# The order of all work in a gated SSM-convolution and GLU kernel, laid out anew

## The chip, the cores and the metric

The kernel runs on one core of a Trainium2 chip. The core has five engines that each work through a queue of their own in order: TensorE (PE, with its weight loads PEld), VectorE (DVE), ScalarE (ACT), GpSimd (POOL) and SyncE (SP). SP and POOL issue the transfers between the chip's memory and the buffers on the core. The metric is the device time of one execution in microseconds, the median over several runs.

## The reference

The inputs are one sequence of 2048 rows by 512 columns (u, also used as x) and the weights of two branches, which a gate mixes:

```python
x = A_u
g = _sigmoid((x * gate_w).sum(-1, keepdims=True))
a = _A_ref(x, ...)     # diagonal SSM as a long convolution
b = _B_ref(x, B_w_gate, B_w_up, B_w_down)
return g * a + (1 - g) * b
```

Branch A has 512 channels with 128 complex states each. It builds a kernel of length 2048 for every channel and convolves it with the input:

```python
logdA, dB = dt * A, dt * Bc
P = jnp.exp(logdA[:, :, None] * l[None, None, :])
K = jnp.einsum("dn,dnl,dn->dl", Cc, P, dB).real
y = irfft(rfft(pad(u)) * rfft(pad(K)))[:L] + u * Dskip
```

Branch B is a gated linear unit of width 1792: `h = _sigmoid(x @ w_gate) * (x @ w_up)`, then `h @ w_down`.

## The kernel before

**The gated unit.** The 2048 rows are worked in two halves of two blocks of 512; the 1792 columns in 14 tiles of 128, in groups of 3, 4, 4 and 3. Every float32 operand is split into a high and a low part in a reduced format, and three products (high-high, high-low, low-high) are summed. `split` (L1022) does this for x, for the gate and up weights and for the down weights: it takes a staging buffer `st`, loads 256 KB into it from SP's queue, and its inner part `halves` has ScalarE write the high part (L1031) and VectorE the low part (L1032). `load_x` (L1008), `load_gu` (L1041) and `load_dn` (L1065) call it. `hidden` (L1083) runs the gate and up products on TensorE (L1098). `post` (L1137) has ScalarE take the tanh (L1141), VectorE multiply by the up product (L1143), and both split the result into `h` (L1147, L1148). `down` (L1153) multiplies `h` with the down weights into the bank `dps` (L1170), and `add` puts the result out: the first group by a store from SP, later ones by a store from POOL that adds in memory (L1194), the last two groups of the rows 8 to 15 by VectorE into a buffer that is read back and stored at the end (`take`, L912).

**The SSM kernel.** The channels are worked in 16 groups of 32, two to a table. `powers` (L484) and `angles` (L514) make sines, cosines and exponentials on ScalarE and VectorE; `magnitudes` (L533) builds one factor `B` of the kernel table, `tables` (L581) the other, `T`, by repeated doubling on VectorE (`double`, L561, with L575 to L577), and multiplies the two on TensorE in bursts of 128 small matmuls (`kps`, L619), one burst per group. `sort` copies the result, `second` (L631) does the first step of its Fourier transform (`wps`, L649), copies it into `kev` on ScalarE (L658) and stores 1 MB to `a_k` from SP (L661). Eight such stores are made, four for each half j of the channels.

**The convolution.** `rows` (L671) reads u, takes the gate's dot products (`dot`), does the first step of u's transform (`ups`) and stores to `a_u` (`urest`, L734). `passes` (L750) runs over j = 0 and 1. For j it waits until the four stores of that half are planned, and then in four rounds loads a part of `a_u` (four loads), does the second step (`ustep`, L804, `s2u`), loads parts of `a_k`, transforms and multiplies (`kstep`, L832, `s2k`, twice in a round), does the first step back (`inverse`, L866, `ips`), copies out (`evict`, L888) and stores to `b_s`. `finals` (L929) reads `b_s` back once a half's stores are done, and `last` (L944, `fps`) does the last step, scales by the gate and adds to the output, by POOL's adding stores or into the buffers of `take`.

**What sets the order.** Each of these is a Python generator that yields its next instruction (or short run of instructions) with the engine it goes to. `Plan.run` (L250) picks one at a time and appends it to that engine's queue; which one comes next is read from the string ORDER (L66). A letter stands for a pair of a kind of work and an engine through LETTERS and TURNS (L56, L57), and takes the first instruction of that kind that is pending for that engine. For work that may go to ScalarE or VectorE, the letter also chooses the engine. The plan's durations enter the program only where a free buffer is chosen. Letters that the text uses:

- Z `hidden` (six matmuls; the first eight three), a `down` (three matmuls), U `tables` on TensorE (128 small matmuls), l `second` on TensorE, n its store on SP, m its copies on ScalarE
- E, D, F loads of gate and up weights, of x and of down weights on SP; f/g, d/e, h/i their splits on ScalarE/VectorE
- S `tables`, Q `mags`, N `angles`, K `powers` on VectorE; R, P, M `mags`, `angles`, `powers` on ScalarE
- u/v `post` on ScalarE/VectorE; y `add` on POOL; z `add` on VectorE; r/s `urest` copies on ScalarE/VectorE
- b loads of `passes` on SP; 1 `ustep`, 5 `kstep`, 8 `inv`, & `last` on TensorE; 2/3 `ustep` copies, !/# `evict` copies, (/) `last` on ScalarE/VectorE; 6 `kstep` on VectorE; $ `evict` stores and 9 loads of `finals` on SP; * `last` on POOL; c `take` on SP

Of the kernel before, what the change touches and what calls it, by code (L numbers as in the profile page):

```python
# [33 lines left out]
L, D, F = 2048, 512, 1792  # L34
# [29 lines left out]
         "kstep -", "kstep PE", "kstep DVE", "inv -", "inv PE", "finals SP", "evict ACT", "evict DVE",  # L64
         "evict SP", "last -", "last PE", "last ACT", "last DVE", "last POOL")
ORDER = (  # L66
    "ABDdeEfgZZEfGDdBgeZZEfgDdeZGVEfZBgDdeZWZWEfpgZZFDEudWfgZZhepvpAuvEWfEgZZDfCHugZZHpqXDIDJvIFdeZuKFdeiuhadeZKZLZMKvivahZMZ"
    "MNOMMGPXVEfKMuNPviuaSZwSZxPSSSvuSSZSPYVSvSSuQgRSSaaZZaEZfvwZgZauaSaSvRQrtxHuEZQZQvQwZtZaaSuuENOZPaZfvSNxSSTfrYVgEutPwKvE"
    "tWWUZZPvGHffPoaKLMQgZZZgZEKppuvuMRWWfpFuZvZaEfRpqMvMgZaZQQQuMurQTNOwUPZZKNMSutSvShoaaSaPSPSivSSuSZZPwaaaZZuSrgQRESjkwlvg"
    "StaaxaESxFRESxmfxQZwZfhaQQivvugQtmZZFhExgSNOSuPfZZavvuNnviZSgaZFEEhPituvaSSPZTwyUPuoZaaXQaIaRJXVIKHKwyZaRQLafMKaafZguwyv"  # L70
    "gUaaZaMQMYVQQNfZaOZTMuMKrvtvPNMwyuvSgSSKSKrZtEEYZtVtWWPWSSWuvPoaaaaZSjkPLSQSfrtMKtwyaupSpSZRSvMSfRQQQSSQSggNaaZurawtMZMy"
    "lmamtaZaOawyZZuESvvaZFPNpSphiSTavXFEaPuauZwyZPUPQXvZuvRZRQQQhQuFTZMKZoZhEENOVYZZVHrFtutrUvtMSPNSoZtfgfgSjSfZuvSZSiigaPkS"
    "hvPYVaZSuWZSPuvQSRRviSaaZSpSQwynZrWutWErtEttWQSfSZagZvQpuaaQSpNpSOawylaaaaZmuPNwPyZSPfaaXaSTawyPmZXVZUQogIvZuaaaJIKKaYst"
    "tZRwyaaaaLMKRQQQQrNTOVMfvnMtHZMwyMKgYPNUotauMSSKSSPSZPSZrPaDDSDjtSakrluZtZKvQSRRvSZZaSvZSQtZmmQdtQuvDuQNOnbbbbbb0veSuZwa"
    "ayavZZZPuNdePFuP1bb2ZSSvShvuaSiSdPFZSTZLM3ewUy45uKMFdhohvvubeZZaZZQRR6bub4MbZbH5iavZqDia6QZbQQQNOTuZMMPDdwyUZ6NKvPvMSSSS"
    "oaaSSubDdeajSZPSkuPdlZ6Swaa7eZuQSSmabbmb8DdnyRveSeZv!RSZZvE0!$wa$ZuuSQQQQSNOS!!$$ESyZaaw1baaaP2ZZuNPSSTwUbv345vZyPEbvZfg"
    "PQoaaaZZuvR6bRIbJ4u6bIKQbZbuQKLMywZaQaa5fgwQKMZaaT6MvaNObyM67wZU8fMKPoavqyNMaaSKZSSSjkPZSgwEaFaKxaEGfSub!vSuZ!$$SPSSgbyw"
    "aaPZSuQZSaS!b!x$vvSRlZRQQuvufQQSZwamLMKaaZmuNEMhOf0Sw1b$b3MSxZPNMgSvaZxaaZ24SgvZ56bbEPPTb4wbUZPZQuMuZZboababRRu5Z6ZaivEv"
    "KQbZQZbEbQQTv6xNOEwU67fgx8ZuMnPfNoaufaaZSSSSvgS!uZSP!$$vSvPwaaSaZSZESPSQgFuvhixSjSfFuvZSRZRgZQuvS!hQkQ!FhlZiQiZufgwaaamv"
    "NamnZSwaaaOPNP$aESuvP$SST0wP1bbZyZxUQuvoRRQQQQZaa2fgaZaZTuvZ34ZwUoj5bEb66akuvbb4auvaZawlmmnbbbbZZZuvbab56aZZyfEug6bvbbbZ"  # L80
    "7b8E#u!Eb#b$b$bav#Zfgbawuv013344$Zaaa56$56b66bZbb9buZE9bZy90bZafwbb71bb3g9Zu24bay8!b!Z$ZEfvf#4v#g%$05b66bEaZbZuE5bbg6vbb"
    "b&($bbZ)bb)f((**(6(**gZ0Za199f22a99Z$ZwauFaugv193399a7fvuEFaZu8!#4Z9hvg4Z$!%u$i%#5F&(6))((**fZZEbvu$f(h6g$999g(w&))b5v**"
    "ZiZuZb4Zav)((*9%*((hy**FcZha667iZbu&()i5)((**ca((**bcbZazZcaa6avaz8!!!6$aaaazZc#v4Z566$aubauauy7Zaz8a!ya$v#u$c!av!aZzaav"
    "$$Zavu$azZu$999aaa9%ZZc&()aycZaZua9aFaF)v(v(**F999%&9h99u(9%&ia(*zvvu(h*vhiazia99aaaa()aaza)(a(az)z*99))c)%&a)c)cz(ca)a)"
    "z)c)*aaaa(a(a*z))acaazczc*")

XLATE = 0
SLACK = dict(dma=1.6, eng=0.06)
# [226 lines left out]
def body(ctx, tc, xp, xt, prm, ldt, dsk, gw, wgu, wdn, c_wu, c_wf, c_wk, c_wwk, c_wwu, c_wwv, c_pw, out):  # L315
# [53 lines left out]
    g = cst.tile([P, NM], F32, name="g")  # L369
# [10 lines left out]
    E = {n: Ev() for n in ("dt", "pw", "wu", "gwb", "wk", "wf", "dsk")}  # L380
# [627 lines left out]
    def load_x():  # L1008
        for half in range(2):
            for sb in range(2):  # L1010
                if (half, sb) == (0, 1):
                    yield begun_w[0, XLATE]
                xsl, = yield X_, 1
                x = xsl.tile("x")
                xready[half, sb][1] = x, xsl
                o = half * HALF + sb * 512
                for dc in range(NC):
                    if (half, sb, dc) == (0, 0, 1):
                        yield first_w
                    yield from split("split", xt[dc, :, o:o + 512], x[:, 0, dc], x[:, 1, dc], xsl, xready[half, sb][0][dc])  # L1020

    def split(kind, src, hi, lo, slot, ready):  # L1022

        s, = yield ST, 1
        n = math.prod(hi.shape[1:])
        flat = s.tile("st")[:, :n]
        st = flat if len(hi.shape) == 2 else flat.rearrange("p (a b) -> p a b", a=hi.shape[1])
        t = yield "SP", kb(n / 2), lambda: S.dma_start(flat if len(src.shape) == 2 else st, src), [s.t]

        def halves():  # L1030
            te = yield "ACT", act(n) + 0.04, lambda: A.activation(hi, st, AF.Copy), [t, slot.t]  # L1031
            te = yield "DVE", dve(n), lambda: V.tensor_tensor(lo, st, hi.bitcast(F32), op=OP.subtract), [te]  # L1032
            s.free(te)
            ready.set(te)
        plan.spawn(halves(), kind)

    def drop(slot, used):
        yield used
        slot.free(used.t)

    def load_gu():  # L1041
        for half in range(2):
            for n, f in enumerate(SLICES[half]):
                if half == 1 and n < KEEP:
                    wready[1, f][1] = wready[0, f][1]
                    for k in range(2):
                        wready[1, f][0][k].set(0.0)
                    plan.spawn(drop(wready[1, f][1][1], wready[1, f][2]), "free")
                    continue
                gs, = yield GUW, 1  # L1050
                gu = gs.tile("gu")
                wready[half, f][1] = gu, gs
                if half == 1 or n < NF - KEEP:
                    plan.spawn(drop(gs, wready[half, f][2]), "free")
                for k, ready in enumerate(wready[half, f][0]):
                    if (half, f) == (0, 0):
                        src = wgu[f].rearrange("p (k c m) -> p k c m", k=2, c=NC)[:, :, k]
                        yield from split("splitw", src, gu[:, 0, :, k], gu[:, 1, :, k], gs, ready)
                        if k == 0:
                            first_w.set(0.0)  # L1060
                        continue
                    yield from split("splitw", wgu[f, :, 512 * k:512 * k + 512], gu[:, 0, k], gu[:, 1, k], gs, ready)
                begun_w[half, f].set(0.0)
# [138 lines left out]
    for gen, kind in ((steps(), "steps"), (const("pw", pw, c_pw.to_broadcast([P, NA + NS + 32]), kb(490)), "pw"),  # L1202
                      (load_x(), "x"), (load_gu(), "w"), (load_dn(), "dn"), (const("wu", wu, c_wu.rearrange("p (c r k) -> p c r k", c=2, r=2), kb(64)), "const"),
                      (const("gwb", gwb, gw.to_broadcast([P, D]), kb(560)), "const"), (preludes(), "preludes"), (powers(), "powers"),
                      (angles(), "angles"), (magnitudes(), "mags"), (tables(), "tables"),
                      (rows(), "rows"), (const("wk", wk, c_wk, kb(128)), "const"),
                      (const("dsk", dskt, dsk.rearrange("p (g s) -> p g s", g=NG), kb(64)), "const"),
                      (const("wf", wf, c_wf.rearrange("p (q m) -> p q m", q=2), kb(32)), "const"), (hidden(), "hidden"), (down(), "down"), (passes(), "passes"), *((take(t), "take") for t in range(8, NM))):
        plan.spawn(gen, kind)
# [58 lines left out]
```

## Time and profile before

| What | Value |
|---|---|
| Median of 3 runs | 648.88 us (645.97 to 654.21) |
| Profiled execution | 644.45 us |
| Its span, first to last instruction | 642.7 us |
| Mean granted TensorE clock | 0.984 |
| Bytes moved by transfers | 105.50 MB, mean 164 GB/s |
| Matmuls of `hidden` (L1098) and `down` (L1170) | 1344 and 672 |

The span is cut into 40 slices of 16 us in the page's second part, where each digit is the busy share of a slice in tenths. A wait is idle time of an engine just before an instruction, with what ended it. A window row sums an engine's busy time between two points of the span. The DMA share is the mean busy share of the core's 16 DMA engines, as the view prints it (it can read a little above 1).

### The profile page before, as it was taken

The page shows a single profiled execution, that of the slowest core. Times are in us where ns is not written, and L with a number is a line of the kernel's source. Part 1 is how long each engine was busy: PE and PEld are TensorE (multiplying, and loading weights), DVE is VectorE, ACT ScalarE, POOL GpSimd, SP SyncE. Part 2 cuts the span into 40 slices and gives each one's busy share as a digit, 9 for nine tenths or more (in the row PEclk, how much of TensorE's full clock was granted, in tenths as well). Part 3 has the DMA queues.
Part 4 walks back from the last instruction along what each step waited for, and adds up shares of the span by engine and source line. Part 5 has one row for each costly group of instructions (what it writes and reads, how often), then busy time and mean ns, then how long its engine had stood idle before and what let it go on. Part 6 is the DMA issues. An engine that isn't in the chain of part 4 may idle for free.

```text
span 642.7 us, 16774 instructions
## 1 busy us (share of the span) xinstructions
PE 603.5 (94%) x7145; PEld 451.9 (70%) x7145; DVE 548.5 (85%) x784; ACT 431.3 (67%) x650; POOL 49.9 (8%) x61
## 2 busy tenths in 40 slices
PE   7999989899998997998999999989999987998987
PEld 3667778677876875866776777767776664676755
DVE  5999889999999999999999899998657652985367
ACT  4595998789898599789966899587642332442130
POOL 0000000011100110000010100000100010242021
PEclk9999999999999899899999999999999987999989
DMA  7504624439634628589488346735489999998986
GB/s 246 174 33 115 197 68 160 143 48 229 149 100 157 164 35 234 161 179 210 96 165 173 69 124 157 217 105 156 72 193 253 233 240 276 256 208 187 239 177 164
DMA packets 94650, 105.50 MB, mean 164 GB/s; under 512 B 39664, under 2 KB 65136, under 8 KB 93552
## 3 DMA queue, kind: packets, MB, share of 16 engines
q1 hardware_dynamic: 86512, 92.89, 53.1%
q0 software_dynamic: 8064, 11.54, 13.0%
q8 instruction: 56, 0.92, 0.6%
q14 instruction: 18, 0.15, 0.1%
HBM read 61.41 MB, written 42.99 MB: 162 GB/s over the span
## 4 chain that ended last, share of the span: by engine, by line
DVE 37%; PE 24%; ACT 14%; DMA 13%; issue 7%; SPq 4%; POOL 1%; DVEq 0%; POOLq 0%; ACTq 0%
PE gups L1098 10%; PE dps L1170 9%; DVE t L575 3%; DVE T L576 3%; DMA parts<-b_s 3%; DVE T L577 3%; DVE h L1148 2%; DVE sg L1143 2%; DVE gu L1032 2%; ACT B L547 2%; DMA parts<-a_u 2%; DVE B L556 2%; DMA st<-wgu 2%; DVE dnw L1032 2%; DVE ex L475 2%
## 5 line engine op out<-in xcount | busy, mean ns | idle before, releaser
L1098 PE MATMUL gups<-x,gu 128*128 128x512 f32 x1344 | 338.2, 399 | 5.7 <-ACT sg L1141 1.5
L1098 PEld LDWEIGHTS gups<-x,gu 128*128 128x128 f32 x1344 | 251.4, 190 | 77.3 <-issue 8.5
L1170 PE MATMUL dps<-dnw,h 128*128 128x512 f32 x672 | 176.8, 400 | 6.0 <-DVE h L1148 2.8
L1170 PEld LDWEIGHTS dps<-dnw,h 128*128 128x128 f32 x672 | 125.6, 190 | 45.2 <-issue 7.5
L1194 POOL DMA_DIRECT2D out<-part x31 | 27.8, 896 | 452.1 <-ACT part L1189 437.9
L1147 ACT ACTIVATE h<-sg 128x512 fp32r<-128x512 f32 x56 | 34.7, 627 | 32.7 <-DVE sg L1143 18.6
L547 ACT ACTIVATE B<-B 128x32 f32<-128x32 f32 (+2 forms) x96 | 53.5, 672 | 0.3
L1189 ACT ACTIVATE part<-dps,omg 128x512 f32<-128x512 f32 x47 | 32.0, 682 | 22.6 <-PE dps L1170 22.4
L1148 DVE TENSOR_TENSOR h<-sg,h 128x512 fp32r<-128x512 f32 x56 | 38.2, 684 | 7.6 <-ACT h L1147 7.5
L575 DVE TENSOR_TENSOR t<-T,bz 128x1024 f32<-128x1024 f32 (+3 forms) x48 | 41.2, 859 | 1.9 <-ACT ez L479 0.7
L577 DVE TENSOR_TENSOR T<-T,t 128x1024 f32<-128x1024 f32 (+3 forms) x48 | 41.5, 864 | 0.7
L1143 DVE SCALAR_TENSOR_TENSOR sg<-sg,gups 128x512 f32<-128x512 f32 x56 | 37.5, 679 | 5.3 <-ACT sg L1141 5.3
L576 DVE TENSOR_TENSOR T<-T,bz 128x1024 f32<-128x1024 f32 (+3 forms) x48 | 41.3, 860 | 0.0
L619 PEld LDWEIGHTS kps<-B,T 128*32 128x32 f32 x2048 | 29.4, 110 | 12.2 <-ACT part L1189 9.7
L1031 ACT ACTIVATE gu<-st 128x512 fp32r<-128x512 f32 (+1 forms) x49 | 29.1, 606 | 12.2 <-DMA st<-wgu 12.0
L619 PE MATMUL kps<-B,T 128*32 128x64 f32 x2048 | 31.9, 220 | 5.3 <-ACT part L1189 4.9
L1032 DVE TENSOR_TENSOR gu<-st,gu 128x512 fp32r<-128x512 f32 (+1 forms) x49 | 32.0, 661 | 3.0 <-ACT gu L1031 3.0
L1141 ACT ACTIVATE sg<-gups 128x512 f32<-128x512 f32 x56 | 33.1, 591 | 0.8 <-PE gups L1098 0.6
L658 ACT ACTIVATE kev<-wps 128x1024 f32<-128x1024 f32 x16 | 30.9, 2003 | 3.1 <-PE wps L649 3.1
L340 ACT ACTIVATE ev<-ips 128x512 f32<-128x512 f32 x23 | 13.2, 597 | 27.9 <-PE ips L879 19.9
L479 ACT ACT_TABLE_LOAD x23 | 29.5, 1283 | 0.4
L340 ACT ACTIVATE yt<-fps 128x512 f32<-128x512 f32 x7 | 4.2, 597 | 32.2 <-PE fps L954 32.2
(129 smaller groups left out, 728.7 us busy)
## 6 DMA issues: line engine op xcount, KB each, us to landing
st<-wgu SPq DMA_DIRECT2D x45, 256.0 KB, 4.8
a_u<-evu SPq DMA_DIRECT2D x32, 256.0 KB, 4.3
a_k<-kev SPq DMA_DIRECT2D x8, 1024.0 KB, 4.9
b_s<-ev SPq DMA_DIRECT2D x32, 256.0 KB, 4.4
out<-part POOLq DMA_DIRECT2D x31, 256.0 KB, 4.4
ak<-a_k SPq DMA_DIRECT2D x28, 256.0 KB, 6.1
parts<-b_s SPq DMA_DIRECT2D x24, 256.0 KB, 8.0
st<-wdn SPq DMA_DIRECT2D x23, 256.0 KB, 4.7
```

The source lines that it names most:

```text
L547: A.activation(B[:, :, 0, 1 << k::2 << k], B[:, :, 0, 1:64 >> k:2], AF.Exp, scale=float(1 << k))
L575: yield "DVE", c, lambda: V.tensor_tensor(t2, src, sb, op=OP.mult), [t, slot.t]
L576: te = yield "DVE", c, lambda: V.tensor_tensor(dst, src, br, op=OP.mult), [t]
L577: te = yield "DVE", c, lambda: V.tensor_tensor(dst, dst, t2[:, :, ::-1], op=OP.add), [te]
L619: mm(p[32 * jj:32 * jj + 32, s], T[:, 32 * i + ch, c], B[:, ch, c], start=(c == 0), stop=(c == 1), tile_position=(0, 32 * jj), skip_group_ ...
L1032: te = yield "DVE", dve(n), lambda: V.tensor_tensor(lo, st, hi.bitcast(F32), op=OP.subtract), [te]
L1098: mm(p, gu[:, a, k, dc], x[:, b, dc], start=(dc + n == 0), stop=(dc == NC - 1 and n == 2))
L1141: t = yield "ACT", ("exp", actp(512)), lambda: A.activation(sg, pg_, AF.Tanh, scale=0.5), [tg, ss.t]
L1143: t = yield "DVE", dve(512), lambda: V.scalar_tensor_tensor(sg, sg, 1.0, pu, op0=OP.add, op1=OP.mult), [t, tu]
L1147: t = yield "ACT", act(512), lambda: A.activation(h[:, 0], sg, AF.Copy), [t, hs.t]
L1148: t = yield "DVE", dve(512), lambda: V.tensor_tensor(h[:, 1], sg, h[:, 0].bitcast(F32), op=OP.subtract), [t]
L1170: mm(p, h[:, a, 128 * s:128 * s + 128], dn[:, b], start=(f == fs[0] and n == 0), stop=(f == fs[-1] and n == 2))
```

## The change

ORDER is replaced as a whole by another string of the same length; the operations stay the same. In `split`, the number of elements is no longer taken from the shape of the destination but from a new argument, 512 unless given, and `load_gu` gives 256 for the four pieces of the first block. That number sets the size of the staging buffer and of the load, and the durations with which the plan books the two halves of the split. Of both strings the last lines are shown, from the line with the sixteenth U on; the thirteen lines ahead of them are left out.

```diff
 ORDER = (
...
-    "NamnZSwaaaOPNP$aESuvP$SST0wP1bbZyZxUQuvoRRQQQQZaa2fgaZaZTuvZ34ZwUoj5bEb66akuvbb4auvaZawlmmnbbbbZZZuvbab56aZZyfEug6bvbbbZ"
-    "7b8E#u!Eb#b$b$bav#Zfgbawuv013344$Zaaa56$56b66bZbb9buZE9bZy90bZafwbb71bb3g9Zu24bay8!b!Z$ZEfvf#4v#g%$05b66bEaZbZuE5bbg6vbb"
-    "b&($bbZ)bb)f((**(6(**gZ0Za199f22a99Z$ZwauFaugv193399a7fvuEFaZu8!#4Z9hvg4Z$!%u$i%#5F&(6))((**fZZEbvu$f(h6g$999g(w&))b5v**"
-    "ZiZuZb4Zav)((*9%*((hy**FcZha667iZbu&()i5)((**ca((**bcbZazZcaa6avaz8!!!6$aaaazZc#v4Z566$aubauauy7Zaz8a!ya$v#u$c!av!aZzaav"
-    "$$Zavu$azZu$999aaa9%ZZc&()aycZaZua9aFaF)v(v(**F999%&9h99u(9%&ia(*zvvu(h*vhiazia99aaaa()aaza)(a(az)z*99))c)%&a)c)cz(ca)a)"
-    "z)c)*aaaa(a(a*z))acaazczc*")
...
+    "OfmSSZwyamnZaZP1bbNSSSaPZSgTPawUuPQgvZuEZoaRaRQQaZQEQTya2fEuZv345bbbwyb6E6Uo$Zvj$kaaa4ufauwlmgZZaZZ5vgmavuZZuEEnbbbbbbbb"
+    "b6bbybv67Z8!##a0bawZuf#v13Z244f5vu656Z$b$bbbb6Za67$$b0uZaZa8f!!!bZuEg9bv#gf1999b%$3vbZb24$b56g&(v))awbZb4(fb6gZZuva56(*6"
+    "*Eb0b9$Z(bb9bbb(*a*aZa1$fwgb32456ZgZ6E7b8!E#au!v9uv4ZF9%au!vb$Zfg$9$hifZ9Fb9&))b5b9Zu$60Zau)(9(**((*v6Fb9ga99huvviZZ%w12"
+    "*Zu%&(b3v)Z)((b4FZaa**&)(hi(*Zb7aZ*))hZ5((bciZ6uvZa**((8!z!aaZ**b46acyaz!!$56$6b7aaaZa8cz$#!c$$a$uv!!$uvaya$cuvZ9caZyzaa"
+    "cuaazvZ9aaauaZvuz9aavaaz9%&)y)Z)9a9cu9ZaFhi(9%(*9F9hai*F&)((*azvhi9Zu*9%)aa9a9aaa9vu&()9(av(zz)a)aa)ca%z*a)a)c&zc)caaa(a"
+    "*())))a)azc)azcaaazcazc(**")
...
@@ -1019,10 +1019,9 @@
                         yield first_w
                     yield from split("split", xt[dc, :, o:o + 512], x[:, 0, dc], x[:, 1, dc], xsl, xready[half, sb][0][dc])
 
-    def split(kind, src, hi, lo, slot, ready):
+    def split(kind, src, hi, lo, slot, ready, n=512):
 
         s, = yield ST, 1
-        n = math.prod(hi.shape[1:])
         flat = s.tile("st")[:, :n]
         st = flat if len(hi.shape) == 2 else flat.rearrange("p (a b) -> p a b", a=hi.shape[1])
         t = yield "SP", kb(n / 2), lambda: S.dma_start(flat if len(src.shape) == 2 else st, src), [s.t]
@@ -1055,7 +1054,7 @@
                 for k, ready in enumerate(wready[half, f][0]):
                     if (half, f) == (0, 0):
                         src = wgu[f].rearrange("p (k c m) -> p k c m", k=2, c=NC)[:, :, k]
-                        yield from split("splitw", src, gu[:, 0, :, k], gu[:, 1, :, k], gs, ready)
+                        yield from split("splitw", src, gu[:, 0, :, k], gu[:, 1, :, k], gs, ready, 256)
                         if k == 0:
                             first_w.set(0.0)
                         continue
```

More of the change, by code (lines that the diff above doesn't have):

```diff
@@ L66 @@
 ORDER = (
[L67 to L78, printed above, removed]
@@ L79 @@
-    "KQbZQZbEbQQTv6xNOEwU67fgx8ZuMnPfNoaufaaZSSSSvgS!uZSP!$$vSvPwaaSaZSZESPSQgFuvhixSjSfFuvZSRZRgZQuvS!hQkQ!FhlZiQiZufgwaaamv"
-    "NamnZSwaaaOPNP$aESuvP$SST0wP1bbZyZxUQuvoRRQQQQZaa2fgaZaZTuvZ34ZwUoj5bEb66akuvbb4auvaZawlmmnbbbbZZZuvbab56aZZyfEug6bvbbbZ"
-    "7b8E#u!Eb#b$b$bav#Zfgbawuv013344$Zaaa56$56b66bZbb9buZE9bZy90bZafwbb71bb3g9Zu24bay8!b!Z$ZEfvf#4v#g%$05b66bEaZbZuE5bbg6vbb"
-    "b&($bbZ)bb)f((**(6(**gZ0Za199f22a99Z$ZwauFaugv193399a7fvuEFaZu8!#4Z9hvg4Z$!%u$i%#5F&(6))((**fZZEbvu$f(h6g$999g(w&))b5v**"
@@ L83 @@
-    "ZiZuZb4Zav)((*9%*((hy**FcZha667iZbu&()i5)((**ca((**bcbZazZcaa6avaz8!!!6$aaaazZc#v4Z566$aubauauy7Zaz8a!ya$v#u$c!av!aZzaav"
-    "$$Zavu$azZu$999aaa9%ZZc&()aycZaZua9aFaF)v(v(**F999%&9h99u(9%&ia(*zvvu(h*vhiazia99aaaa()aaza)(a(az)z*99))c)%&a)c)cz(ca)a)"
-    "z)c)*aaaa(a(a*z))acaazczc*")
+    "ABEfgBDdeZZEGfDdBgeZZEfDdGVWpeWpEfWgZDdZpgeZZWpXAEfgDdZZEefguZZqvuEFHHCIJvDhfdIiaKgZEfZuKLMKMFvgZZeZDdMuXFNOVYeMDhMKdPeZ"
+    "viauZZvZEMZhNEuSViSSvaSPuZvZPurPttfrYSuZwaaaEtFfStZSVKWvWKSSQRSZRgSSvLMwaaaSgGHZSQZEufxErtWQKMMQSZQvNEWHxwaaauZZOuZZPfMS"
@@ new lines @@
+    "hfSpSNPvZZSTgvwUZuvpgPGZxpxEufPQuZRgpvRZvZigqoaaaQZruuZQQQTvvNOtwEtMKufUgPNMSSSZufvSgSEZSoPaaavSSZPZEtPuQSZvuZSRvZjSuSZR"
+    "QkQwaaaQvZuQSwxNOlaaFaFhhZvPxFSiSNZEZSfwaufhvxEiPZuSXvPamgZaZZZSiEuPEvfZuSTawyZUxXVmfYgZgVQoIaZrutaagJIHKKRvLMvKaRQQQQNO"
+    "wyuvMZMMaaaawyfgMKPTZNauaaawyHfgvZUZMSSSEnturtZYVPKSKLoaaPMaErtSaSvSjWWkZSfWPSWuKSQpgSSvZSrlwyRZRQQQQMSNOuvpaZZaaaSmMZmt"
+    "wytPuZtEvpESapNaauvaZSSwyaaFFfgMPSTafPFaPuvhiZZZZFwyUZXQhiuvoZRaZZEEZXVRQQfuvufZZMQhihiuvYVvaaZQuTuvvawygtUNOPKMgNSfZrtt"
@@ new lines @@
+    "gSSoSjSSSgkaSZSrYttVWPWWPZPEEaaSQWaSSuvnwyZSRRpQSQQrQpZatautaaSwyZNvOSpSSaaaZrtlPmfNpSauvXgXwyTZfZaPaZaaZPuwUmZPQouZnIJa"
+    "aVyYRgIvKKLaZtRQMKZDruDtQMaZDZQQvdTMwyUMNOMPvKeNDodMSudeSPrZtvVPSKSjkSStKPuSeZaSSvSQYaaawyruRZSaRFShvSQaiFtatFtQZQZaQHud"
+    "vZrNOuevwyZhhlmmZPSNiSiuZZZZaaSLSDdttuZZPuSPMKDdPSTawyvZvMvUQMeDnbbbbbb01bbdMDeuvMKeZRRQQQQuv2ZoZMuNOZaa245b6bb4qbbHaTbZ"
+    "dZwyPNUP5bbboaZ6baSjkPSPu6aSQRSRveSwyS6SQSlmSQS7vQZmuvQSNZOaZaZaEEfwuv8!F!$$0SyuvfSaZPgSZSNhSaawyuvZSaSaiST!!q12bb$2ZZEP"
@@ new lines @@
+    "Zu4awyEgZP5bbbbbbb4U6PQZuEovavIa6Ra$JwIyZuRQQaKuKvfZaZ5bZEbabZuLMKQMMMQTn6wZyMZUNfOPKZugNMSgfSSZ67SvSoSjaaaPPvkPQSvSwx8!"
+    "!u$Z$SgRESaaKaZSZRQQQSvZ!SQZuSwxaaEaNSOfu0!wxlZa$aamZmn1bbKPuSZNSZSgSTwUxfvg2EvvPP245LMKbbb4bPQuv6Zfgoaauav6ZRRQQwMuZMZx"
+    "bEMaQQNO$MKa5awbxbvbZfaPaNfgau6ZTwUbPZMSxZ678PSSSvSoSaPQauFbgZSajvZ!!0$$hSSiRuSvSRQQk!ZZwFauvQ!ZFhSiZauhiZluvQxGEfaaSEvN"
+    "OfmSSZwyamnZaZP1bbNSSSaPZSgTPawUuPQgvZuEZoaRaRQQaZQEQTya2fEuZv345bbbwyb6E6Uo$Zvj$kaaa4ufauwlmgZZaZZ5vgmavuZZuEEnbbbbbbbb"
```

## The prediction

> **What bounds the kernel now.** I read the page first, then the windows by stage, then the timeline of TensorE in the last stage, then the groups for prices. The page:
>
> ```profile
> span 642.7 us, 16774 instructions
> PE 603.5 (94%) x7145; PEld 451.9 (70%) x7145; DVE 548.5 (85%) x784; ACT 431.3 (67%) x650; POOL 49.9 (8%) x61
> DVE  5999889999999999999999899998657652985367
> ACT  4595998789898599789966899587642332442130
> DMA  7504624439634628589488346735489999998986
> ```
>
> Two stages show. In the first 70% of the span VectorE is full, slice after slice, and DMA is half idle; then VectorE falls off and DMA is full. TensorE's 94% says little: its busy time runs on while a matmul waits for its weights. Windows cut at the last table group and the last `wps` group say it in numbers (busy us and count of PE, PEld, DVE, ACT, POOL; clock; DMA share; GB/s):
>
> ```profile
> 20.00:440.00 420.00, 401.23 (x4916) 308.75 (x4915) 407.18 (x573) 351.50 (x518) 21.02 (x24) 0.99 0.54 139
> 440.00:462.00 22.00, 20.86 (x271) 16.14 (x269) 15.38 (x16) 16.27 (x23) 2.61 (x3) 1.00 0.65 149
> 470.00:591.00 121.00, 112.59 (x1412) 78.56 (x1397) 77.46 (x102) 40.41 (x70) 18.53 (x21) 0.96 1.05 231
> 591.00:643.00 52.00, 45.23 (x290) 32.91 (x289) 29.41 (x48) 12.19 (x24) 7.03 (x8) 0.96 0.80 196
> ```
>
> From 20 to 440 us VectorE idles 420 - 407.2 = 12.8 us, and from 440 to 462 another 6.6. So the sixteenth table group (letter U), which needs all tables, comes when VectorE has got through what stands before it. From 470 to 591 us the DMA share is 1.05: the second half of the passes (j=1), its reads and writes and the output, is held by transfers. The landmarks in the timeline of TensorE, with its waits for transfers:
>
> ```profile
> 461.98 1.99 PE L619 MATMUL kps<-B,T 128*32 128x64 f32 x128
> 469.23 2.10 PE L649 MATMUL wps<-wk,kst 32*64 32x128 f32 x128
> 502.21 0.71 PE L817 MATMUL s2u<-parts,wwu 32*32 32x256 f32 x28 [0.54 <-DMA parts<-a_u]
> 518.67 0.66 PE L954 MATMUL fps<-parts,wf 64*32 64x256 f32 x14 [2.62 <-DMA parts<-b_s]
> 534.36 0.62 PE L817 MATMUL s2u<-parts,wwu 32*32 32x256 f32 x4 [2.02 <-DMA parts<-a_u]
> 535.36 0.71 PE L817 MATMUL s2u<-parts,wwu 32*32 32x256 f32 x28 [0.39 <-DMA parts<-a_u]
> 536.62 0.87 PE L817 MATMUL s2u<-parts,wwu 32*32 32x256 f32 x4 [0.54 <-DMA parts<-a_u]
> 537.76 1.15 PE L817 MATMUL s2u<-parts,wwu 32*32 32x256 f32 x28 [0.27 <-DMA parts<-a_u]
> 618.76 1.10 PE L954 MATMUL fps<-parts,wf 64*32 64x256 f32 x14 [0.77 <-DMA parts<-b_s]
> 630.33 8.45 PE L1170 MATMUL dps<-dnw,h 128*128 128x512 f32 x36
> ```
>
> U16 runs at 462.0 us, the last `wps` (l8) at 469.2 us, and some 173 us follow it.
>
> **The change part by part.** The new argument of `split` gives the value that the removed line worked out (512, and 256 for the first block of gate and up weights), so the two edits there alter no instruction. What remains is the order string. Counted letter by letter, both strings have 2186 letters and the same number of each, apart from the engine of a few copies: `urest` one from VectorE to ScalarE, `ustep` four from VectorE to ScalarE, `evict` three from VectorE to ScalarE, `last` three from ScalarE to VectorE. So nothing is added; the cost lies in where things stand. The prices:
>
> ```profile
> L340 DVE COPY uf<-s2u 128x1024 f32<-128x1024 f32 x4 | 4.9, 1217 | 0.0
> L340 DVE COPY evu<-ups 128x1024 f32<-128x1024 f32 x1 | 1.2, 1224 | 0.0
> L340 ACT ACTIVATE uf<-s2u 128x1024 f32<-128x1024 f32 x6 | 6.0, 1016 | 2.4 <-issue 1.8 <-PE s2u L817 0.6
> L855 DVE TENSOR_TENSOR uf<-s2k,uf 128x1024 f32<-128x1024 f32 x10 | 12.2, 1224 | 0.3
> L861 DVE TENSOR_TENSOR uf<-tt 128x512 f32<-128x512 f32 x10 | 6.9, 692 | 0.3
> L1143 DVE SCALAR_TENSOR_TENSOR sg<-sg,gups 128x512 f32<-128x512 f32 x56 | 37.5, 679 | 5.3 <-ACT sg L1141 5.3
> ```
>
> (1) VectorE ahead of U16. Before minus after, by letters ahead of the sixteenth U: `ustep` copies 4 become 1 (-3 x 1.22 = -3.66), the `urest` copy goes (-1.22), one `post` instruction moves behind (-0.68), and one whole `kstep` product moves ahead (two instructions of 1.22 and two of 0.69: +3.83). Sum -1.7 us on the engine that sets this stage, on the path. ScalarE gets there three `ustep` copies, one `urest` copy of 1.02 each and one split more, +4.7 us; in 20 to 440 it is idle 420 - 351.5 = 68.5 us, which hides it. If that cover failed, the 4.7 would fall on VectorE's waits.
>
> (2) VectorE's idle time in that stage. Its waits before 460 us are small ones for ScalarE:
>
> ```profile
> DVE B L552 <- ACT B L547: 3.6, 3, 2.9
> DVE ex L475 <- ACT af L474: 2.6, 2, 1.5
> DVE B L541 <- PE kps L619: 2.0, 1, 2.0
> ```
>
> The new order interleaves `mags`, `angles` and `powers` on ScalarE in another way, and no row shows which waits come of it. Bounds: all idle time of 20 to 462 goes, -19.4; as much again comes, +19.4. The longest single row is 2.9 us, and the same producers and consumers stay, so I take 0.
>
> (3) Transfers behind l8. Ahead of l8 now stand three more loads of gate and up weights (9 after it become 6) and two more accumulating stores of `out<-part` on POOL (7 become 5); all other SP and POOL letters after l8 agree in number.
>
> ```profile
> st<-wgu SPq DMA_DIRECT2D x45, 256.0 KB, 4.8
> out<-part POOLq DMA_DIRECT2D x31, 256.0 KB, 4.4
> parts<-a_u SPq DMA_DIRECT2D x16, 256.0 KB, 5.7
> ak<-a_k SPq DMA_DIRECT2D x28, 256.0 KB, 6.1
> a_k<-kev SPq DMA_DIRECT2D x8, 1024.0 KB, 4.9
> ```
>
> Five times 256 KB is 1.31 MB; at 231 GB/s 5.7 us, in a stage whose share is 1.05, moved into one whose share is 0.54. Bounds: 0 (latency, not volume, holds the tail) and -5.7. I take -5.7, as the share row is nearest.
>
> (4) The distance from load to use in j=1. Two steps of the chain of waits price TensorE's steady work:
>
> ```profile
> 455.93 1.36 PE gups L1098 x6
> 457.29 0.68 PE dps L1170 x3
> ```
>
> With 1.36 us for each Z and 0.68 for each a (and 1 to 2 us for a burst of small matmuls, as in the landmarks), the work between the fourth `a_u` load of a round and its `ustep`, summed over the letters, was 10.5, 6.1, 13.6 and 9.6 us before; after it is 5.5, 8.9, 4.8 and 6.8. A landing takes 5.7, so two rounds fall short, by 0.2 and 0.9; with 0.4 for the clock below, +1.5. Bounds: -3.8 (the waits of 0.54 at 502 and of 2.02, 0.39, 0.54 and 0.27 at 534 to 538 go) and +19 (each of four rounds waits a whole landing, 22.8, less those 3.8).
>
> (5) SP's queue at the eighth `second` store (n). Two weight loads (EE) now stand between the copies that fill `kev` and that store. Behind it on SP wait all loads of j=1, and for those the first `kstep` of j=1 on TensorE.
>
> ```profile
> SPq L1028 <- DVE gu L1032: 20.2, 8, 8.0
> ```
>
> ```profile
> L658 ACT ACTIVATE kev<-wps 128x1024 f32<-128x1024 f32 x16 | 30.9, 2003 | 3.1 <-PE wps L649 3.1
> ```
>
> TensorE has 18.7 us of work from l8 to that `kstep`, 19.4 before. The chain that it covers is 4.0 + 4.9 + 6.1 = 15 us (two copies of 2.0, then the write of `a_k` and its read). A weight load that blocks SP for up to 8.0 us breaks the cover: bounds 0 and 15 + 8.0 - 18.7 = +4.3. I take 0, since the mean of those blocks is 2.5 and fits.
>
> The rest (rows of `u` earlier, down projections spread otherwise, single engine swaps after l8, where VectorE idles a third) has the bound of (2) and is taken at 0. TensorE's own work is the same. Sum: -1.7 + 0 - 5.7 + 1.5 + 0 = -5.9 us. Against the profiled execution's 644.45 that is 638.5. The median of the runs, 648.88, stands 0.7% above it; in that measure 643.0.
>
> **The clock.** Waits of TensorE cost twice:
>
> ```profile
> 520.00:525.00 5.00, 5.00 (x17) 3.99 (x16) 2.45 (x4) 1.15 (x4) 0.00 (x0) 0.68 1.19 236
> 535.00:540.00 5.00, 3.83 (x63) 1.65 (x64) 0.97 (x1) 0.00 (x0) 0.00 (x0) 0.69 1.11 289
> 540.00:545.00 5.00, 5.00 (x66) 3.61 (x73) 1.98 (x3) 1.12 (x2) 0.00 (x0) 0.63 1.11 269
> ```
>
> Right after the wait of 2.62 us the granted clock is 0.68 for 5 us, a loss of 1.6; after the broken waits at 534 to 538 it is 0.69 and 0.63, a loss of 3.4. The Trainium skill, "TensorE: Matmul & The Clock Gate", Part 1, says that the clock is halved after an idle window of about 3.4 us and comes back after about as long a busy one. The trace agrees that idleness lowers it, but a wait of 2.62 us on top of slow small matmuls was enough here. By that rule of the Trainium skill the shortfalls of (4) would cost no clock, and the sum would be -6.3.
>
> **The rivals.**
> Faster: (2) goes to its good end. For it speaks that 19.4 us of idle VectorE lie where it is the bound; against it, that they are in many pieces of under 3 us. With three quarters gone, 644.45 - 5.9 - 14.6 = 624, or 628 in the median's measure.
> Slower: the waits of (4). Each of the four rounds of j=1 finds its `a_u` load not landed, for its whole 5.7 us, and pays 1.6 to 3.4 of clock: 4 x (5.7 + 2.5) = 33, less the 3.8 and 3.4 shown now, +26. With (1) and (3), 663, or 668 in the median's measure. For it speak the shorter distances, and a DMA share over 1, in which landings stretch; against it, that SP runs ahead of the other engines, so that the letter's place is not the time of issue. It decides from about three full waits on.
> No change: the tail is held by the chain load, `kstep`, `inv`, `b_s`, last stage and not by volume, so (3) is 0 and the times agree: 644.45 - 0.2, or 649.
>
> **How the numbers follow.** The forecast with its own range (637 to 651) and the no-change case lie within 2%, which is about what a measurement of this kernel can tell from no change: 635.9 to 661.9. Chances: forecast 0.40, no change 0.23, faster rival 0.23, slower rival 0.14. So faster by over 2% 0.23, within 0.63, slower 0.14. The range of 8 in 10 reaches most of the way to the faster case and partly to the slower: 629 to 657.
>
> **What would show it.** (1) U16 starts at 460 +/- 5 us and VectorE's idle time from 20 to 440 is 8 to 18 us. (3) The time from l8 to the end is 166 to 172 us and the share in it stays near 1. (4) `s2u` on TensorE waits 3 to 6 us for `parts<-a_u` in j=1; over 15 us means the slower rival. (5) `s2k` waits under 1 us for `ak`. U16 before 450 us means the faster rival; the forecast is wrong in kind if U16 moves by over 10 us either way, or the tail by over 12.

## The result and the profile after

| | Before | After |
|---|---|---|
| Median | 648.93 us (645.97 to 654.21, 4 runs) | 624.19 us (622.58 to 627.87, 4 runs) |
| Ratio | | 0.962, 95% interval 0.954 to 0.969 |
| Profiled execution, span | 644.45 us, 642.7 us | 622.58 us, 620.8 us |
| U16 starts at (time from U1 to U16) | 461.98 us (392.7 us) | 446.14 us (375.9 us) |
| From l8 to the end of the span | 173.5 us | 168.3 us |

A second measurement of the changed kernel gave 625.40 us and a ratio of 0.964 (0.962 to 0.967). The change is faster by 3.8%, outside the range of 629 to 657 us. The time is near that of the faster rival (628 us); whether its mechanism came too is told below. The page of the changed kernel:

```profile
span 620.8 us, 16791 instructions
PE 596.6 (96%) x7145; PEld 449.9 (72%) x7145; DVE 540.8 (87%) x779; ACT 433.1 (70%) x653; POOL 49.9 (8%) x61
DVE  5999999999999999999999999999756666765467
ACT  3799986999986699998978979986643333523030
DMA  7618342177543936585858546645499999999996
PE 50%; DVE 17%; ACT 15%; DMA 10%; issue 4%; SPq 2%; DVEq 0%; ACTq 0%
```

The first five rows look like those of before, VectorE full and then DMA. The last row, which gives the shares of the chain that ended last by engine, does not. The page of before has there:

```profile
DVE 37%; PE 24%; ACT 14%; DMA 13%; issue 7%; SPq 4%; POOL 1%; DVEq 0%; POOLq 0%; ACTq 0%
```

TensorE's share of the chain has doubled and VectorE's has halved, at the same operations. The windows up to U16, first of before, then of after (columns as above: busy us and count of PE, PEld, DVE, ACT, POOL; clock; DMA share; GB/s):

```profile
0.00:462.00 462.00, 437.72 (x5237) 334.09 (x5237) 434.60 (x627) 376.18 (x554) 24.36 (x32) 0.99 0.55 144
```

```profile
0.00:446.10 446.10, 433.84 (x5259) 333.78 (x5259) 427.08 (x623) 378.57 (x557) 24.35 (x32) 1.00 0.56 149
20.00:440.00 420.00, 413.23 (x5173) 321.62 (x5172) 408.90 (x576) 366.53 (x536) 22.75 (x26) 1.00 0.56 147
```

Nearly the same matmuls are done 15.9 us sooner. TensorE's idle time falls from 24.3 to 12.3 us, and VectorE's from 27.4 to 19.0. So 12.0 of the 15.9 us are idle time of TensorE; the other 3.9 are its busy time, at a granted clock of 0.99 before and 1.00 after. VectorE's busy time falls by 7.5, of which some 4.9 are the four copies that left it. In the window of 20 to 440 us TensorE does 5173 matmuls where it did 4916, while VectorE is as full as before (408.9 us beside 407.2). So the page's "VectorE is full" was true of both kernels and did not say what held the first one.

The waits of TensorE up to 446 us (engine, line and tile, what it waited for: us in all, times, longest), before and after:

```profile
PE kps L619 <- ACT part L1189: 3.7, 3, 1.9
PE dps L1170 <- DVE h L1148: 2.8, 3, 1.7
PE wps L649 <- ACT evu L340: 2.0, 2, 1.4
PE wps L649 <- ACT ev L340: 2.0, 2, 1.4
```

```profile
PE dps L1169 <- ACT part L1188: 2.5, 3, 1.5
PE gups L1097 <- DVE x L1031: 2.0, 1, 2.0
PE kps L619 <- ACT part L1188: 1.8, 3, 0.8
```

The rows for `wps` and `h` are gone and those for copies that free a bank (`part`) are a little shorter (L1097, L1169, L1188 are L1098, L1170, L1189 of before). No single row is worth the result; many short waits went.

The tail, TensorE's waits behind U16, of before and after:

```profile
PE fps L954 <- DMA parts<-b_s: 5.2, 6, 2.6
PE s2u L817 <- DMA parts<-a_u: 3.8, 5, 2.0
PE s2k L844 <- ACT ev L340: 1.7, 1, 1.7
```

```profile
PE s2k L844 <- issue: 4.0, 1, 4.0
PE dps L1169 <- DVE parts L1182: 2.5, 2, 2.1
PE fps L954 <- DMA b_in<-b_s: 0.4, 1, 0.4
```

The waits for reads of `b_s` and `a_u`, 9.0 us, are down to 0.4; others took 6.5 in their place. In a second profiled execution of the changed kernel (after_again) the waits for these two reads are 2.5 us.

### The profile page after: what moved, and what is told of

Its sections match the earlier page's. It is cut to its first block, busy times and chain, and to the rows that moved or that the text cites. A ratio compares the mean times of both kernels' runs of the same rounds, so it can differ in the third digit from the quotient of the medians.

```text
span 620.8 us, 16791 instructions
## 1 busy us (share of the span) xinstructions
PE 596.6 (96%) x7145; PEld 449.9 (72%) x7145; DVE 540.8 (87%) x779; ACT 433.1 (70%) x653; POOL 49.9 (8%) x61
## 4 chain that ended last, share of the span: by engine, by line
PE 50%; DVE 17%; ACT 15%; DMA 10%; issue 4%; SPq 2%; DVEq 0%; ACTq 0%
PE gups L1097 26%; PE dps L1169 15%; PE kps L619 2%; ACT B L547 2%; DMA st<-wgu 2%; DMA b_s<-ev 2%; PE s2k L844 2%; ACT L479 2%; PE wps L649 2%; PE ips L879 2%; DVE t L575 2%; DMA st<-wdn 2%; DVE T L576 2%; DMA b_in<-b_s 1%; DVE T L577 1%
## 5 line engine op out<-in xcount | busy, mean ns | idle before, releaser
L1097 PE MATMUL gups<-x,gu 128*128 128x512 f32 x1344 | 336.9, 398 | 5.2 <-DVE x L1031 2.0
L1097 PEld LDWEIGHTS gups<-x,gu 128*128 128x128 f32 x1344 | 251.3, 190 | 74.7 <-issue 9.1
L1169 PE MATMUL dps<-dnw,h 128*128 128x512 f32 x672 | 176.1, 399 | 6.0 <-ACT part L1188 2.5
L1169 PEld LDWEIGHTS dps<-dnw,h 128*128 128x128 f32 x672 | 124.6, 189 | 45.9 <-issue 10.5
L1193 POOL DMA_DIRECT2D out<-part x30 | 26.3, 886 | 432.2 <-ACT part L1188 416.3
L340 ACT ACTIVATE ev<-ips 128x512 f32<-128x512 f32 x26 | 14.6, 597 | 43.7 <-PE ips L879 39.6
L1188 ACT ACTIVATE part<-dps,omg 128x512 f32<-128x512 f32 x46 | 31.3, 681 | 14.4 <-PE dps L1169 13.4
L1030 ACT ACTIVATE gu<-st 128x512 fp32r<-128x512 f32 (+1 forms) x51 | 30.9, 609 | 9.2 <-DMA st<-wgu 8.8
L1031 DVE TENSOR_TENSOR gu<-st,gu 128x512 fp32r<-128x512 f32 (+1 forms) x51 | 33.9, 665 | 1.7 <-ACT gu L1030 1.7
L1030 ACT ACTIVATE dnw<-st 128x512 fp32r<-128x512 f32 x24 | 14.8, 626 | 13.9 <-DMA st<-wdn 10.3
```

The lines of the kernel that those rows point to most:

```text
L1097: mm(p, gu[:, a, k, dc], x[:, b, dc], start=(dc + n == 0), stop=(dc == NC - 1 and n == 2))
L1169: mm(p, h[:, a, 128 * s:128 * s + 128], dn[:, b], start=(f == fs[0] and n == 0), stop=(f == fs[-1] and n == 2))
```

## The experiments

Below, "U1 to U16" is the time between the starts of the first and the sixteenth table burst on TensorE. It is used beside U16 itself, since the same front started U1 at 70.3, 71.2 and 73.4 us in three profiled executions, but took 375.9, 377.0 and 377.0 us from there to U16. The old front took 392.7 and 395.1 us in two executions, so a difference of 2 to 3 us between single profiles says little.

### Which stage holds the gain

Two kernels join the strings at the sixteenth U.

```diff
-ORDER = new
+ORDER = new[:U16] + (what is left of the operations, in old order)   # front_new_tail_old
+ORDER = old[:U16] + (what is left of the operations, in new order)   # front_old_tail_new
```

> The new order up to the sixteenth U, then the old order of what is left. Theory A (the gain of some 22 us of span lies mostly ahead of U16, and the two stages add up): U16 at 446 us as in the changed kernel, the rest 181 us as before, so a span near 627 and a ratio of 0.975. Rival (the tail's gain is due to a start that the front sets up, or the front's gain is eaten in the tail): a ratio at 0.962 or above 0.985.

> The old order up to the sixteenth U, then the new order of what is left. Theory A: U16 at 462 us as before, then 175 us as in the changed kernel, so a span near 637 and a ratio of 0.991. Rival (the transfers moved ahead of l8 made the tail's gain, and here they are still behind it): no gain, a ratio of 1.0.

| | Ratio (95% interval) | U1 to U16 | l8 to the end |
|---|---|---|---|
| front_new_tail_old | 0.979 (0.973 to 0.985) | 377.0 us | 177.3 us |
| front_old_tail_new | 0.990 (0.984 to 0.996) | 395.1 us | 167.8 us |

Both parts gain on their own, as theory A said, and the product of the ratios, 0.969, is close to the whole. The new front takes 375.9 and 377.0 us with either tail, and the old one 392.7 and 395.1. The old tail gives some of it back: it takes 177.3 us behind the earlier start, 3.8 more than behind the old front. Its waits on TensorE behind U16 show why:

```profile
PE s2u L817 <- DMA au<-a_u: 5.0, 1, 5.0
PE fps L954 <- DMA parts<-b_s: 3.8, 4, 2.7
```

The reads of `a_u` and `b_s` are again what it waits for. This kernel has as few transfers behind l8 as the changed one (6 weight loads, 5 adding stores), and still the old tail's waits. The other kernel doesn't test the rival that was set against it: its three weight loads and two adding stores come between U16 and l8, so they too stand ahead of l8, and not behind it as the expectation assumed.

### Is VectorE's work the bound

Step (1) priced work on VectorE. Four copies ahead of U16 change engine, and nothing else.

```diff
-... s ... 3 ... 3 ... 3 ...      # urest, ustep copies on VectorE
+... r ... 2 ... 2 ... 2 ...      # the same on ScalarE (old_copies_act)
```

new_copies_dve is the reverse in the new order; there the plan's choice of a free buffer also differs from one point on (the two `xb` buffers that TensorE writes are exchanged).

> The old order with four copies ahead of U16 (three of ustep, one of urest) on ScalarE in place of VectorE, nothing else changed. Theory B (VectorE's work bounds the front, so its 4.9 us less count in full): U16 near 457 us, ratio 0.992. Rival (ScalarE's queue is as tight, and its 4.1 us more come back as waits of TensorE for banks): U16 within 1 us of 462 or later, ratio 1.0 or above.

> The new order with the same four copies put back on VectorE. Theory B: U16 near 451 us, a span of 625 to 626 and a ratio of 0.970. Rival: U16 stays at 446 and the ratio at 0.962.

Measured: old_copies_act 1.007 (1.003 to 1.010), U1 to U16 397.3 us, 4.6 longer. new_copies_dve 0.967 (0.961 to 0.972), U1 to U16 381.4 us, 5.5 longer than in the changed kernel. In the old order theory B fell: with less work on VectorE it is slower, by 0.3 to 1.0%. The window of 20 to 440 us shows TensorE behind that of before:

```profile
20.00:440.00 420.00, 396.72 (x4880) 305.24 (x4882) 398.64 (x563) 350.22 (x518) 21.02 (x24) 0.99 0.55 139
```

VectorE's 8.5 us less are in part work that has not been reached by 440 us; counted up to each kernel's own U16, its busy time falls by 4.1 us (434.6 to 430.5). In the window TensorE's waits of `kps` for `part` grew from 3.7 to 5.4 us and those of `dps` for `part` from 0.2 to 2.4. One place shows how: ScalarE's queue stands 2.47 us for the input of the copy that was moved to it, and TensorE then waits for the copy behind it, which frees a bank.

```profile
238.88 1.03 ACT L340 ACTIVATE evu<-ups 128x1024 f32<-128x1024 f32 x1 [2.47 <-PE ups L704]
242.53 3.02 PE L1170 MATMUL dps<-dnw,h 128*128 128x512 f32 x12 [2.22 <-ACT part L1189]
```

In the kernel of before that `part` starts at 238.86 us, here at 241.83. So here it counts where an instruction stands, more than the engine's total.

In the new order the numbers are close to what theory B forecast (U16 near 451 us, 0.970), but they don't decide. The ratio's range, 0.961 to 0.972, overlaps that of the changed kernel. Of the 5.5 us, 3.4 lie between the tenth and the eleventh burst, U10 and U11 (39.0 us, beside 35.6), where TensorE waits for a read:

```profile
PE s2k L844 <- DMA ak<-a_k: 2.6, 1, 2.6
```

The changed kernel has no such wait in its two profiles, but new_loads_late2 (below), with the copies where the changed kernel has them and the same order up to there, has 1.4 us of it. That the four copies are wrong in the old order on ScalarE is shown; that they are right there in the new order is not.

### Do the splits' durations make the difference

How the old string was made is not shown. One guess is that it was laid out as though the splits took almost no time, since the change touches the number by which the plan books them; in the two programs that number is the same (512, or 256 for the first block). If the guess is right, the old order should fit a kernel whose splits do take little. Once a buffer has been filled, the splits work on 32 columns, and the rest of each split is left out; both queues keep their order.

```diff
-            te = yield "ACT", ..., lambda: A.activation(hi, st, AF.Copy), ...
-            te = yield "DVE", ..., lambda: V.tensor_tensor(lo, st, hi.bitcast(F32), op=OP.subtract), ...
+            te = yield "ACT", ..., lambda: A.activation(part(hi), part(st), AF.Copy), ...
+            te = yield "DVE", ..., lambda: V.tensor_tensor(part(lo), part(st), part(hi).bitcast(F32), op=OP.subtract), ...
```

The control shortens in the same way the two halves of `h` in `post`, which have the same size and which the change doesn't touch (old_small_h, new_small_h).

> The old order; once a buffer has been filled, the splits of x, gate, up and down weights work on 32 columns in place of 512 (the rest of the split is left out), so 56 of the 76 splits ahead of U16 are short. Each saves some 0.58 us of VectorE and 0.5 of ScalarE, some 32 and 28 us ahead of U16. Theory S (the old order is laid out as if these splits took no time, and the waits come from their real durations): the old order gains much more than the new, U16 at 428 to 436 us, beside 426 to 434 in the new. Rival R (the order is better whatever the splits take): the 16 us between the two stay, U16 near 436 to 440 here and 422 in the new.

> The new order with the same short splits. Theory S: U16 within 5 us of that of the old order with short splits. Rival R: 12 us or more earlier than it.

> Control: the old order, splits of weights and x whole, but the two split instructions of post (the halves of h, of the same size, 86 of them to a kernel ahead of U16 with the tanh and product) work on 32 columns once a buffer has been filled (the rest is left out): some 35 short pairs ahead of U16, some 20 us less of VectorE. Theory S: both orders gain alike, and the new stays 10 us or more ahead at U16. Rival L (any work taken from VectorE and ScalarE closes the gap, weight and x splits are nothing special): the gap at U16 closes to under 6 us.

> The same control in the new order. Theory S: U16 10 us or more ahead of the old order with short halves of h. Rival L: under 6 us ahead.

| | U16 | U1 to U16 | Against the whole kernel of that order | Span | Ratio to before (95% interval) |
|---|---|---|---|---|---|
| old_small_splits | 447.07 us | 378.3 us | -14.4 us | 628.9 us | 0.972 (0.965 to 0.979) |
| new_small_splits | 447.07 us | 376.7 us | +0.8 us | 625.5 us | 0.960 (0.951 to 0.969) |
| old_small_h | 455.67 us | 386.1 us | -6.6 us | 640.4 us | 0.989 (0.982 to 0.995) |
| new_small_h | 446.99 us | 377.1 us | +1.2 us | 622.2 us | 0.961 (0.954 to 0.968) |

With short splits the two orders reach U16 at the same time: theory S and not rival R. But S had both orders at some 430 us, and the new order gained nothing. The timeline and the window of new_small_splits:

```profile
447.07 1.99 PE L619 MATMUL kps<-B,T 128*32 128x64 f32 x128 [0.47 <-DVE B L556]
```

```profile
20.00:440.00 420.00, 412.45 (x5169) 322.29 (x5169) 383.20 (x576) 343.78 (x536) 22.77 (x26) 1.00 0.56 147
```

VectorE is 25.7 us less busy there than in the changed kernel's row, ScalarE 22.8 us, and TensorE has done 5169 matmuls beside 5173. Some 2.7 us of the time are again a wait for `ak` between U10 and U11 (1.9 us, and the slower matmuls behind it). Without it the new order would have gained some 2 us. What is left is TensorE's own queue, busy 412 of 420 us; that this is what holds the front now is argued, as no run shortened it. The same window of old_small_splits:

```profile
20.00:440.00 420.00, 407.74 (x5148) 316.85 (x5147) 391.49 (x583) 341.81 (x535) 22.76 (x26) 1.00 0.56 146
```

That is 232 matmuls more than in the old kernel with whole splits.

The control came out between the theories. The gap from U1 to U16 is 9.0 us, where S wanted 10 or more and L under 6. VectorE's busy time over the whole kernel fell by 23.2 us with short h (548.5 to 525.3) and by 35.2 with short splits (to 513.3), so the old order gained 0.28 us for each microsecond in the one case and 0.41 in the other. With a scatter of 2.4 us between two executions of the old front these two can't be told apart: work of another kind helps too, and whether less is open. So it is shown that taking the splits' time away closes the whole gap, and that the old order suffers from VectorE and ScalarE running late where the new one does not. That the splits alone are behind it, or how the old string was made, is not shown.

### Which of the two engines is late

> The old order; of each split of x and weights only ScalarE's high half is short (32 columns once a buffer has been filled), VectorE's low half is whole. Both halves short moved U16 from 462 to 447 us. Theory Q (the unbooked time in ScalarE's queue delays the copies that free banks for TensorE): most of it, U16 at 450 to 453. Rival V (VectorE's queue is what runs late): U16 at 459 or later.

> The old order; only VectorE's low half of each split is short, ScalarE's high half is whole. Theory Q: little, U16 at 457 or later. Rival V: most of the 15 us, U16 at 449 to 453.

```diff
-A.activation(part(hi), ...); V.tensor_tensor(part(lo), ...)
+A.activation(part(hi), ...); V.tensor_tensor(lo, ...)          # old_short_act
+A.activation(hi, ...);       V.tensor_tensor(part(lo), ...)    # old_short_dve
```

U1 to U16 was 388.1 us with ScalarE's half short (-4.6) and 387.2 us with VectorE's (-5.5), ratios 0.992 (0.989 to 0.995) and 0.984 (0.978 to 0.991). Neither theory holds. Each alone brings about a third of the 14.4 us that both bring. The sum of the two, 10.1, is 4.3 short of that; with single profiles that scatter by 2.4 us, it is likely and not sure that the effects don't add. Rows of old_short_dve show where the rest stays, first its window up to U16, then VectorE's largest waits there:

```profile
0.00:456.50 456.50, 437.17 (x5235) 335.04 (x5235) 409.07 (x628) 375.84 (x554) 24.36 (x32) 0.99 0.56 145
DVE B L552 <- ACT B L547: 7.0, 8, 2.9
DVE x L1041 <- ACT x L1040: 4.5, 5, 1.9
```

In the kernel of before, up to its U16, these two waits are 3.6 and 2.3 us. VectorE is 25.5 us less busy than there (409.1 beside 434.6), and its idle time is 47.4 us where it was 27.4: 5.5 us of the relief reach U16, and 20 become idle time in which VectorE waits for ScalarE and others.

### Is the tail held by the volume behind l8

```diff
-... E ... E ... E ... y ... y ... l   (up to 150 letters ahead of l8)
+... l y y E E E                       (behind l8)
```

> The new order, but three loads of gate and up weights (E) and two adding stores (y) of ahead of l8 stand behind it, so that as many transfers follow l8 as in the old order. Theory of step 3 (the volume behind l8 holds the tail): from l8 to the end 174 us in place of 168, span near 626, ratio 0.971. Rival (what holds the tail is where TensorE waits for the reads of a_u and b_s, not the volume): 168 to 170 us from l8, ratio 0.962 to 0.965.

The ratio, 0.967 (0.960 to 0.974), stood between the two. The kernel was measured again beside the changed one:

> The changed kernel once more, on the same chip as the next run: U16 at 446 to 448 us, 168 to 170 us from l8 to the end, ratio 0.960 to 0.964. It gives the scatter of the times from l8 to the end.

> The new order with the three weight loads and two adding stores behind l8 again. Theory of step 3 (volume): 172 to 176 us from l8 to the end, 4 to 6 us above the changed kernel beside it. Rival (waits for a_u and b_s, not volume): within 2 us of it.

Five runs each gave 625.40 us, ratio 0.964 (0.962 to 0.967), and 628.66 us, ratio 0.970 (0.967 to 0.972). Putting the five transfers behind l8 costs 3.3 us of the median, so a part of step (3) is real. Where it costs them is open: the two profiled executions took the same time (627.83 and 627.82 us), and differ by 1.2 us from l8 to the end (169.3 and 170.5), less than the expected 4 to 6. The TensorE waits of new_loads_late2 from 440 us on:

```profile
PE s2k L844 <- DMA parts<-a_k: 1.9, 1, 1.9
PE s2k L844 <- DMA ak<-a_k: 1.9, 1, 1.9
PE dps L1169 <- DVE parts L1182: 1.8, 2, 1.5
```

With the old volume, the waits for `b_s` and `a_u` do not come back; a little waiting for `a_k` does, as it does with the new volume (1.5 us in after_again). So both hold: the order of the tail took away the long waits, with either volume, and the place of the five transfers is worth some 3 us.

## Why the prediction was wrong, point by point

**What bounds the front.** This is the step that failed. I took VectorE, busy for 407 of 420 us, as "the engine that sets this stage", and priced the change by what moves on it. The runs: 25.7 us less work on VectorE leaves the new order where it is; in the old order 25.5 us less brings U16 forward by 5.5 us, and four copies less, moved to ScalarE, push it back. Busy time of 97% went along with a queue that others wait on at the wrong places; it was not the bound. The sign that the forecast set for itself says so too: VectorE's idle time from 20 to 440 us is 11.1 us, within its 8 to 18, and U16 moved by 15.8 us all the same. TensorE, set aside with "94% says little", is the engine whose idle time was halved. The Trainium skill, "Perfetto Trace Analysis", Identifying the Most-Contended Engine, takes occupancy as the measure for VectorE and says to optimize the engine with the highest first. The measurement decides here: the occupancy was the same in both kernels (407.2 and 408.9 of 420 us), and 12 of the 16 us lay in TensorE's waits, most of them for short copies and halves on VectorE and ScalarE.

**(1)** Forecast -1.7. The count by letters ahead of U16 was also no count of what had run. VectorE's busy time up to U16 fell by 7.5 us, with 623 instructions beside 627: the four copies are gone, and the `kstep` product that I set against them is not in the difference. But the price itself was wrong in kind, as the copies on their own show: +4.6 us in the old order, where -4.9 were priced.

**(2)** Forecast 0, between -19.4 and +19.4. Measured some -15 to -17 for the front as a whole. The ends held and the value did not. I chose 0 because the longest row was 2.9 us and "the same producers and consumers stay". The pieces were short, as read, but there were many of them and the new order removed them together. The faster rival, given 0.23, had the time nearly right but not the mechanism: it had three quarters of VectorE's idle time go, and 8.4 of 27.4 us up to U16 went. What went was half of TensorE's, 12.0 of 24.3. That its time came so near is luck.

**(3) and (4)** Together forecast -4.2 for the tail; measured -5.2 from l8 to the end. In the second profile it is -4.2, so the sum is right, but by two terms whose errors cancel. The volume was worth some 3.3 us of the median and not 5.7. The distance from load to use, for which I took +1.5, went towards its good end: the 3.8 us of `s2u` waiting for `a_u` went (1.2 in the second profile), and with them most of the `fps` waits for `b_s`. The letters had been summed to 10.5, 6.1, 13.6 and 9.6 us before and 5.5, 8.9, 4.8 and 6.8 after. In the traces the fourth `a_u` load of a round of j=1 is issued 7.9, 3.9, 12.5 and 2.6 us ahead of the first `s2u` matmul before, and 8.6, 11.0, 7.2 and 6.3 after. With a landing of 5.7, the two short rounds of before are those with the waits, and the changed kernel has no such round. So the place of a letter was no measure of the time of issue, as the argument against the slower rival said.

**(5)** Held for the load that it priced: the first `kstep` of j=1 starts at 474.3 us without a wait. Its sign, less than 1 us of `s2k` waiting for `ak`, did not hold: a later one waits 4.0 us. The row names no releaser ("issue"), but the read of `a_k` for it was issued at 501.33 and landed at 510.03 us.

```profile
501.33 2.49 SPq L796 DMA_DIRECT2D parts<-a_k  x2
510.12 2.99 PE L844 MATMUL s2k<-parts,wwk 64*32 64x256 f32 x32 [4.03 <-issue]
```

In the second profile of the same kernel the same burst waits 1.5 us for this read. It cost clock besides. The windows of the changed kernel around it (us, PE busy and count, clock, DMA share, GB/s):

```profile
505.00:510.00 5.00, 1.09 (x63) 0.85 1.08 219
510.00:515.00 5.00, 4.87 (x37) 0.50 1.08 230
515.00:520.00 5.00, 5.00 (x80) 0.96 0.97 256
```

The wait ends at 510.1 us and the 5 us behind it run at a granted clock of 0.50, where the wait of 2.62 us of before was followed by 0.68. That is the loss that step (4) put a price on, in another place.

**The two edits in `split`** were taken to alter no instruction. In both programs the number comes to 512, or 256 for the four pieces of the first block, so the plan makes the same queues with or without them; no run tried them without the string.

## What to carry to other kernels

When two in-order queues are both nearly full and feed each other, do not price a change of order by the work that it moves on the fuller one. Take the waits of the engine that does the irreducible work, here TensorE's 24 us up to U16, add them up, and ask for each what stands ahead of its releaser in that queue. A cheap test of whether a full engine is the bound is to shorten a common instruction on it and see whether the landmark moves; shortened in two orders, it also tells which of them suffers from that engine's running late.

## What was not expected of the hardware

The same queue contents gave U1 at 70.3, 71.2 and 73.4 us in three profiled executions, so a landmark's absolute time has a scatter of some 3 us from the start alone, while U1 to U16 agreed within 1.1 us there and within 2.4 in the old front. A read that TensorE needs between U10 and U11 made it wait for 0 to 2.6 us in runs of the new order, which is a part of such scatter. Relief of one of two alternating engines gave 4.6 and 5.5 us, of both 14.4, so effects of queue lateness need not add.
